# Attention with compressive memory, then a gated feed-forward block: the last steps of the blocks beside the attention are tied behind its last weighting of values

## The chip, the cores and the metric

One core of a Trainium2 chip. The metric is the device time of one execution in microseconds; of several runs the median is given. The profile is of one further execution of the same program. TensorE (PE) has two clock levels, 1.2 and 2.4 GHz; where the profile gives a granted clock, 1.00 is the higher and 0.50 the lower.

## The reference

Inputs are q, k and v of shape (4, 8, 576, 64) in float32, a memory M_prev and z_prev for each head, a gate beta for each head, and three weight matrices.

```python
scores = scale * np.matmul(q, k.transpose(0, 1, 3, 2))      # causal mask, softmax
local = np.matmul(a, v)
q_p = np.where(q > 0, q, np.exp(q) - 1.0) + 1.0
mem_out = einsum('bhsd,bhde->bhse', q_p, M_prev) / (einsum('bhsd,bhd->bhs', q_p, z_prev)[..., None] + 1e-06)
x = g * mem_out + (1 - g) * local                           # g = sigmoid(beta)
x = x.transpose(0, 2, 1, 3).reshape(2304, 512)
out = (silu(x @ w_gate) * (x @ w_val)) @ w_out              # d_ff = 1536
```

## The kernel before, in words

The attention handles sixteen pairs of heads (`Pair`, n = 0 to 15; four pairs make one batch of 576 tokens). Each pair is cut into steps: a1 and a2 make scores and their exponentials, b1 and b2 weight and transpose them, c1 and c2 multiply with the values, d1 and d2 add the part recalled from memory and store x. Every fp32 operand of PE is split into two parts, high and low, so each product takes three matmuls. The list STEPS writes out in which order the steps of pair n and of pair n - 1 are issued; a scheduler then sets the order on each engine by priorities and by its own estimate of times.

x goes to two tensors in memory outside the core, xdh and xdl (`store`, L628), as high and low parts, since the feed-forward block needs all heads of a token. It is loaded back by `load_x` (L190).

The feed-forward block is cut in two. Of its twelve slices of 128 hidden columns the first four (FC1) are done **beside the attention** for tokens 0 to 1535: `moe1` (L216), six blocks of N1 = 256 tokens. A block is ten steps: eight of `up` (L197, twelve matmuls of 256 columns each: gate for slices 0 and 1, value for 0 and 1, the same for 2 and 3), and two of `down` (L210; four slices, three matmuls of 512 columns each), whose sum is scaled by ScalarE (L248) into a tile o, of which there is one, and stored as a partial sum in `part` (L249, on SyncE's queue). Between up and down ScalarE takes Silu (L229), VectorE multiplies (u, L236), GpSimd rounds to the high part (u1h) and VectorE makes the low part (u1l). Steps are issued by `fill` (L641): at each of three places of a pair's round it issues steps up to

```python
want = math.floor(steps * (n * 3 + k - START) / (END - START))
```

with priority P_BES behind the attention; what is left at the end is issued in the loop `for _ in bgen` (L680). A block needs x of its whole batch: blocks 0 and 1 that of batch 0, blocks 2 and 3 that of batch 1 too, blocks 4 and 5 that of batch 2 too.

The **second phase** (L707) takes six chunks of 384 tokens: first the two chunks of tokens 1536 to 2303 with all twelve slices, then the four others with the last eight slices, adding the partial sums. Its weights are loaded and converted by `weights` (L163) on ScalarE and VectorE from the end of the attention on. Its first x, tiles xbh and xbl, are loaded as soon as the first 256 tokens of the last pair are stored (d1 of pair 15). PSUM banks are shared: the second phase's up uses s, g, m and av, its down tr.

Of the kernel before, what the change touches and what calls it, by code (L numbers as in the profile page):

```python
# [20 lines left out]
NP = B * NPAIR  # L21
# [6 lines left out]
N2 = 384  # L28
NT1 = 1536
WSTEP = {2: (0,), 3: (1, 2), 4: (3,)}  # L30
START, END = 14, 53
AHEAD = 1

RANK = {"recall": -50, "c1": 50, "load": 400}
# [26 lines left out]
def attention_moe(ctx: ExitStack, tc: tile.TileContext, qt, kt_, v, m, beta, wg, wv, wo, out):  # L61
    nc = tc.nc
    PE, ACT, DVE, POOL, SP = nc.tensor, nc.scalar, nc.vector, nc.gpsimd, nc.sync
# [12 lines left out]
    part = dram.tile([NT, DM], F32, name="part")  # L76
# [81 lines left out]
            DVE.tensor_copy(gx[rows, :, 4, j], gp[rows, :, j])  # L158
            DVE.tensor_copy(oy[rows, :, 8], sp[rows, :, j])

    wsplit = {}

    def weights(f, wpool, spool, tag, nraw, ntmp, after=None):  # L163
        hi = wpool.tile([128, 1536], F32R, name=f"wh{f}")
# [32 lines left out]
    def up(ps, f, gv, xh, xl):  # L197
        hi, lo = wsplit[f]
        n = 0
        for kk in range(NPAIR):  # L200
            c = slice(gv * 512 + kk * 128, gv * 512 + kk * 128 + 128)
            for wt, xx in ((hi, xh), (hi, xl), (lo, xh)):
                PE.matmul(ps, wt[:, c], xx[:, kk, :], start=(n == 0), stop=(n == 11))  # L203
                n += 1

    def gated(u, g, val):
# [2 lines left out]

    def down(ps, f, uh, ul, first, last):  # L210
        hi, lo = wsplit[f]
        PE.matmul(ps, uh, hi[:, 1024:1536], start=first, stop=False)  # L212
        PE.matmul(ps, uh, lo[:, 1024:1536], start=False, stop=False)  # L213
        PE.matmul(ps, ul, hi[:, 1024:1536], start=False, stop=last)  # L214

    def moe1(pool, t0):  # L216
        held = xb
        if t0 // N1 % 2:
            held = [rot(pool, f"bx{part}", [128, NPAIR, N1], F32R, 1) for part in "hl"]
        xh, xl = load_x(held, t0, N1)  # L220
        us = []
        for f0 in range(0, FC1, 2):
            n = min(2, FC1 - f0)
            g = rot(psG, "g", [128, 512], F32, PS_G).rearrange("p (f c) -> p f c", f=2)
            for f in range(f0, f0 + n):
                up(g[:, f - f0, :], f, 0, xh, xl)
                yield
            u = rot(pool, "u1", [128, 2, N1], F32, 1)
            ACT.activation(u[:, 0:n], g[:, 0:n], AF.Silu, scale=W_ONE)  # L229
            ps = rot(psM, "m", [128, 512], F32, PS_M).rearrange("p (f c) -> p f c", f=2)  # L230
            for f in range(f0, f0 + n):
                up(ps[:, f - f0, :], f, 1, xh, xl)
                yield
            uh = rot(pool, "u1h", [128, 2, N1], F32R, (FC1 + 1) // 2)
            ul = rot(pool, "u1l", [128, 2, N1], F32R, (FC1 + 1) // 2)
            DVE.scalar_tensor_tensor(  # L236
                out=u[:, 0:n], in0=ps[:, 0:n], scalar=W_ONE, in1=u[:, 0:n], op0=ALU.mult, op1=ALU.mult
            )
            split_hi(uh[:, 0:n], u[:, 0:n])
            split_lo(ul[:, 0:n], u[:, 0:n], uh[:, 0:n], "u1")  # L240
            us += [(uh[:, f], ul[:, f]) for f in range(n)]
        for j in range(N1 // 128):
            c = slice(j * 128, j * 128 + 128)
            ps = rot(psM, "m", [128, 512], F32, PS_M)
            for f, (uh, ul) in enumerate(us):
                down(ps, f, uh[:, c], ul[:, c], f == 0, f == FC1 - 1)
            o = rot(pool, "o1", [128, 512], F32, 1)
            ACT.mul(o, ps, W_ONE)  # L248
            SP.dma_start(part[t0 + j * 128 : t0 + j * 128 + 128, :], o)  # L249
            yield  # L250

    xb = [xbp.tile([128, NPAIR, N2], F32R, name=f"xb{part}") for part in "hl"]
# [8 lines left out]
    with tc.tile_pool(name="sb", bufs=1, reuse_waits="tile") as sb:  # L261
# [62 lines left out]
        class Pair:  # L324
# [270 lines left out]
            def c2(self):  # L595
                if self.plain:
                    av = rot(psA, "av", [128, 512], F32, PS_A)[:, 0:320]
                    g = self.g2[0]
                    for kk in range(5):
                        o = max(0, (kk - 2) * 128)  # L600
                        for h in range(2):
                            PE.matmul(  # L602
                                av[:, o:320], self.vz[:, kk, h, :], g[:, kk, h, o:320] if kk < 4 else self.last_keys(g, h),
                                start=(kk == 0 and h == 0), stop=False,
                            )
                    self.recalled(av, 2, 3)
                    self.give(2, av)
                    return
                x = self.x2 = rot(quick[0], "x2", [128, 320], F32, 2)
                for h in range(2):  # L610
                    av = rot(psA, "av", [128, 512], F32, PS_A)[:, 0:320]
                    for kk in range(5):
                        o = max(0, (kk - 2) * 128)
                        for g in self.g2:
                            keys = g[:, kk, h, o:320] if kk < 4 else self.last_keys(g, h)
                            PE.matmul(  # L616
                                av[:, o:320], self.vs[:, h, kk, :], keys,
                                start=(kk == 0 and g is self.g2[0]), stop=(kk == 4 and g is self.g2[1]),
                            )
                    self.joined(x, av, h)  # L620

            def d2(self):
                if not self.plain:
# [59 lines left out]
    with tc.tile_pool(name="stg2", bufs=1, reuse_waits="tile") as stg2, \  # L683
# [23 lines left out]
        for t0 in [N2 * i for i in ORDER]:  # L707
# [21 lines left out]
            for f in fs:  # L729
                pp = []  # L730
                for gv in range(2):
                    ngv[0] += 1
                    ps = banks[nj + ngv[0] % (len(banks) - nj)]
# [75 lines left out]
```

## Time and profile before

| | us |
|---|---|
| median of 3 runs (749.72 to 752.3) | 751.47 |
| the profiled execution | 753.47 |
| its span, first to last instruction | 751.7 |

| engine | busy, us | share of the span |
|---|---|---|
| PE | 693.1 | 92% |
| DVE (VectorE) | 401.7 | 53% |
| ACT (ScalarE) | 332.4 | 44% |
| POOL (GpSimd) | 197.9 | 26% |

The attention ends near 390 us, and what follows is the second phase. Busy time of PE is the time in which a matmul is in work; successive matmuls overlap, so the spacing of their starts tells how fast they go. "L203" is line 203 of the kernel. A wait is named by the instruction that waited and the one that released it.

### The profile page before, as it was taken

The numbers are of one execution on the slowest core, as the hardware profiler recorded it, in microseconds if no ns is written. First come the engines' busy times: TensorE is split into PE (matmuls) and PEld (weight loads), VectorE is DVE, ScalarE is ACT, GpSimd is POOL, SyncE is SP. The second block draws the span as 40 slices with busy tenths as digits, with TensorE's granted clock in tenths as the row PEclk, the third lists the DMA queues.
The fourth block names the chain that finished last, engine by engine and source line by source line (L and its number), as shares of the span: only waits on it lengthen the run. The fifth ranks groups of instructions, "written<-read, shape, count | busy, mean of one in ns | idle before, by whom it ended". The sixth has DMA issues, their size and how long they took to land.

```text
span 751.7 us, 11326 instructions
## 1 busy us (share of the span) xinstructions
PE 693.1 (92%) x4172; PEld 621.6 (83%) x4172; DVE 401.7 (53%) x1042; ACT 332.4 (44%) x737; POOL 197.9 (26%) x264
## 2 busy tenths in 40 slices
PE   4577798999979999899969999999999999999997
PEld 2466676998769997698859999999999999999996
DVE  8887764776876977775736995111111221211212
ACT  5555455667668686576725663211121111111111
POOL 5885943544444553452300000000000000000000
PEclk9789799999989999899988999999999999999999
DMA  9555144230362312401048760300040310400201
GB/s 262 180 169 148 54 124 150 70 114 19 104 197 88 114 39 78 162 33 61 20 156 295 221 226 26 115 1 1 13 156 1 112 57 0 169 1 1 84 1 43
DMA packets 43928, 72.58 MB, mean 97 GB/s; under 512 B 11744, under 2 KB 24544, under 8 KB 43872
## 3 DMA queue, kind: packets, MB, share of 16 engines
q1 hardware_dynamic: 43728, 71.56, 29.4%
q8 instruction: 33, 0.54, 0.3%
q10 hardware_dynamic: 144, 0.29, 0.1%
q14 instruction: 23, 0.19, 0.1%
HBM read 54.54 MB, written 17.30 MB: 96 GB/s over the span
## 4 chain that ended last, share of the span: by engine, by line
PE 70%; DVE 11%; DMA 8%; ACT 6%; issue 2%; POOL 2%; SPq 0%; DVEq 0%; ACTq 0%; POOLq 0%
PE s L203 13%; PE g L203 9%; PE m L203 8%; PE av L203 6%; PE tr L213 5%; PE tr L212 5%; PE tr L214 5%; PE s L396 3%; PE av L616 2%; PE tr L473 2%; DMA xbl<-xdl 2%; PE av L602 2%; PE m L212 2%; DMA xbh<-xdh 1%; PE m L213 1%
## 5 line engine op out<-in xcount | busy, mean ns | idle before, releaser
L743 ACT CAST uh<-u 128x384 fp32r<-128x384 f32 x56 | 28.8, 514 | 109.8 <-DVE u L738 109.8
L213 PE MATMUL tr<-wl,uh 128*128 128x512 f32 x168 | 66.5, 396 | 0.0
L212 PE MATMUL tr<-wh,uh 128*128 128x512 f32 x168 | 66.1, 393 | 0.0
L214 PE MATMUL tr<-wh,ul 128*128 128x512 f32 x168 | 64.7, 396 | 0.0
L738 DVE SCALAR_TENSOR_TENSOR u<-s,u 128x384 f32<-128x384 f32 x23 | 12.8, 557 | 86.9 <-PE s L203 86.9
L396 PE MATMUL s<-kh,qh 64*128 64x128 f32 (+3 forms) x128 | 31.1, 463 | 28.8 <-DVE mx L406 15.2
L410 ACT ACTIVATE pl<-pl,mx 128x384 f32<-128x384 f32 (+1 forms) x64 | 42.6, 667 | 31.3 <-DVE mx L406 31.2
L449 POOL TENSOR_SCALAR pl<-pl,rs 128x384 f32<-128x384 f32 (+1 forms) x64 | 44.4, 712 | 19.9 <-ACT x L500 10.8
L396 PEld LDWEIGHTS s<-kh,qh 64*128 64x128 f32 x128 | 14.0, 207 | 40.3 <-DVE mx L406 18.6
L111 DVE TENSOR_TENSOR ul<-u,uh 128x384 fp32r<-128x384 f32 x56 | 31.2, 557 | 26.7 <-ACT uh L743 26.7
L111 DVE TENSOR_TENSOR g2l<-tr,g2h 128x512 fp32r<-128x512 f32 (+1 forms) x66 | 36.2, 572 | 17.1 <-ACT g2h L455 16.4
L449 POOL TENSOR_SCALAR ps<-ps,rs 128x128 f32<-128x128 f32 (+1 forms) x64 | 27.9, 454 | 61.2 <-DVE rs L446 26.4
L473 PE MATMUL tr<-ident,pl 128*128 128x128 f32 x224 | 39.9, 316 | 3.5 <-POOL pl L449 2.0
L406 DVE CUSTOM_DVE_ANT_0 pl<-s,maskp 128x384 f32<-128x384 f32 (+1 forms) x64 | 37.7, 618 | 9.9 <-PE s L396 9.9
L473 PEld LDWEIGHTS tr<-ident,pl 128*128 128x128 f32 x224 | 29.3, 161 | 10.4 <-POOL pl L449 4.5
L214 PEld LDWEIGHTS tr<-wh,ul 128*128 128x128 f32 x168 | 31.6, 188 | 7.3
L203 PE MATMUL s<-xbh,wh 128*128 128x384 f32 x92 | 32.1, 352 | 4.9 <-DMA xbh<-xdh 4.9
L212 PEld LDWEIGHTS tr<-wh,uh 128*128 128x128 f32 x168 | 31.6, 188 | 5.2
L213 PEld LDWEIGHTS tr<-wl,uh 128*128 128x128 f32 x168 | 31.6, 188 | 5.1
L410 ACT ACTIVATE ps<-ps,mx 128x128 f32<-128x128 f32 (+1 forms) x64 | 28.9, 452 | 13.3 <-DVE mx L406 13.1
L455 ACT CAST g2h<-tr 128x512 fp32r<-128x512 f32 (+1 forms) x66 | 30.5, 494 | 7.0 <-PE tr L473 4.8
L737 ACT ACTIVATE u<-s 128x384 f32<-128x384 f32 x23 | 11.2, 489 | 49.5 <-PE s L203 49.5
(197 smaller groups left out, 2188.2 us busy)
## 6 DMA issues: line engine op xcount, KB each, us to landing
qr<-in_qt_dram SPq DMA_DIRECT2D x16, 384.0 KB, 4.2
out_dram<-pt SPq DMA_DIRECT2D x18, 256.0 KB, 2.2
kr<-in_kt_dram SPq DMA_DIRECT2D x15, 288.0 KB, 3.8
xdh<-xh SPq DMA_DIRECT2D x15, 288.0 KB, 2.6
xdl<-xl SPq DMA_DIRECT2D x15, 288.0 KB, 2.2
wrawb<-in_wg_dram SPq DMA_DIRECT2D x8, 512.0 KB, 4.1
wrawb<-in_wv_dram SPq DMA_DIRECT2D x8, 512.0 KB, 4.4
wrawb<-in_wo_dram SPq DMA_DIRECT2D x8, 512.0 KB, 4.3
```

Of the source, the lines that this page charges most:

```text
L111: return eng.tensor_tensor(dst, src, hi.bitcast(F32), op=ALU.subtract)
L203: PE.matmul(ps, wt[:, c], xx[:, kk, :], start=(n == 0), stop=(n == 11))
L212: PE.matmul(ps, uh, hi[:, 1024:1536], start=first, stop=False)
L213: PE.matmul(ps, uh, lo[:, 1024:1536], start=False, stop=False)
L214: PE.matmul(ps, ul, hi[:, 1024:1536], start=False, stop=last)
L396: mm = PE.matmul(ps[h][:, 0:w], q[rows, t * 128 : t * 128 + 128], k[rows, 0:w], start=(i == 0), stop=(i == 2))
L406: read[id(ps[h])] = DVE.tensor_tensor_reduce(out=p[:, 0:w], in0=ps[h][:, 0:w], in1=maskp[:, 512 - w : 512], op0=ALU.add, op1=ALU.min, scal ...
L410: ACT.activation(p[:, 0:w], p[:, 0:w], AF.Exp, bias=mx[:, c + h : c + h + 1], scale=-1.0, accum_out=self.sm[:, c + h : c + h + 1],)
L449: POOL.tensor_scalar(p, p, rs[:, i : i + 1], 1.0, op0=ALU.mult, op1=ALU.mult)
L455: ACT.copy(view(g[0]), src)
L473: PE.transpose(tr[:, c * 128 : c * 128 + 128], p[:, (k0 + c) * 128 : (k0 + c) * 128 + 128], ident)
L743: ACT.copy(uh, u)
```

## The change

Three things are changed. END goes from 53 to 56, so that `fill` issues the sixty steps over more of the attention. The last matmul of the last pair's c2 is kept (`ends`), and each sum of `up` and each first matmul of `down` that is written after it follows it in PE's order. These are steps 48 to 59, the two downs of block 4 and all of block 5, and also all of the second phase. The store of the partial sum is issued by ScalarE instead of SyncE.

```diff
-START, END = 14, 53
+START, END = 14, 56
...
-    wsplit = {}
+    wsplit, ends = {}, []
...
             for wt, xx in ((hi, xh), (hi, xl), (lo, xh)):
-                PE.matmul(ps, wt[:, c], xx[:, kk, :], start=(n == 0), stop=(n == 11))
+                mm = PE.matmul(ps, wt[:, c], xx[:, kk, :], start=(n == 0), stop=(n == 11))
+                if n == 0 and ends:
+                    follow(mm, ends[-1], "kept for the time that the last x takes to come back")
                 n += 1
...
     def down(ps, f, uh, ul, first, last):
         hi, lo = wsplit[f]
-        PE.matmul(ps, uh, hi[:, 1024:1536], start=first, stop=False)
+        mm = PE.matmul(ps, uh, hi[:, 1024:1536], start=first, stop=False)
+        if ends:
+            follow(mm, ends[-1], "kept for the time that the last x takes to come back")
...
             ACT.mul(o, ps, W_ONE)
-            SP.dma_start(part[t0 + j * 128 : t0 + j * 128 + 128, :], o)
+            ACT.dma_start(part[t0 + j * 128 : t0 + j * 128 + 128, :], o)
...
                         for g in self.g2:
                             keys = g[:, kk, h, o:320] if kk < 4 else self.last_keys(g, h)
-                            PE.matmul(
+                            mm = PE.matmul(
                                 av[:, o:320], self.vs[:, h, kk, :], keys,
...
                     self.joined(x, av, h)
+                if self.n == NP - 1:
+                    ends.append(mm)
```

The scheduler makes a new order of it. Lines of the changed file are some four to six higher than those of before (L620 is L616 before, L214, L217 and L218 are L212 to L214, L477 is L473, L505 is L501, L240 is L236). Numbers behind a name tell buffers apart.

PE, the last pair's transposes of weighted exponentials (tr from p and pl) before, with the end of block 5's first down ahead and the start of its second behind them:

```order
L212 MATMUL m_1119<-wh_870,u1h_1437 128x512
L213 MATMUL m_1119<-wl_871,u1h_1437 128x512
L214 MATMUL m_1119<-wh_870,u1l_1438 128x512
L473 MATMUL tr_254<-ident,p_220 128x128 x4
L473 MATMUL tr_249<-ident,pl_202 128x128 x4
L473 MATMUL tr_259<-ident,p_220 128x128
L212 MATMUL m_1119<-wh_505,u1h_1262 128x512
L213 MATMUL m_1119<-wl_506,u1h_1262 128x512
L214 MATMUL m_1119<-wh_505,u1l_1263 128x512
```

The same place on PE in the changed kernel:

```order
L477 MATMUL tr_249<-ident,pl_357 128x128 x3
L477 MATMUL tr_254<-ident,p_220 128x128 x4
L477 MATMUL tr_259<-ident,pl_369 128x128 x4
L477 MATMUL tr_249<-ident,pl_202 128x128 x4
L513 MATMUL tr_254<-ident,mem_159 128x128 x2
L516 MATMUL tr_254<-fold,mem_159 128x64
L620 MATMUL av_275<-g2h_1229,vs_982 128x320
L477 MATMUL tr_259<-ident,p_220 128x128
L620 MATMUL av_275<-g2l_1230,vs_982 128x320
```

Before, twelve matmuls of down stood on either side of these transposes; now none does, and from the last pair's first scores on PE has the attention's matmuls alone.

PE, the last weighting of values (av, pair 15) and what follows it, before:

```order
L616 MATMUL av_275<-g2h_1229,vs_982 128x320
L616 MATMUL av_275<-g2l_1230,vs_982 128x320
L616 MATMUL av_275<-g2h_1229,vs_982 128x192
L616 MATMUL av_275<-g2l_1230,vs_982 128x192
L616 MATMUL av_275<-g2h_1229,vs_982 128x64
L616 MATMUL av_275<-g2l_1230,vs_982 128x64
L203 MATMUL s_170<-xbh,wh_505 128x384
L203 MATMUL s_171<-xbh,wh_505 128x384
L203 MATMUL g_1042<-xbh,wh_676 128x384
L203 MATMUL m_1119<-xbh,wh_676 128x384
L203 MATMUL av_275<-xbh,wh_699 128x384
L203 MATMUL s_170<-xbl,wh_505 128x384
```

The same place in the changed kernel:

```order
L620 MATMUL av_275<-g2h_1229,vs_982 128x320
L620 MATMUL av_275<-g2l_1230,vs_982 128x320
L620 MATMUL av_275<-g2h_1229,vs_982 128x192
L620 MATMUL av_275<-g2l_1230,vs_982 128x192
L620 MATMUL av_275<-g2h_1229,vs_982 128x64
L620 MATMUL av_275<-g2l_1230,vs_982 128x64
L214 MATMUL m_1173<-wh_505,u1h_1262 128x512
L217 MATMUL m_1173<-wl_506,u1h_1262 128x512
L218 MATMUL m_1173<-wh_505,u1l_1263 128x512
L214 MATMUL m_1173<-wh_676,u1h_1262 128x512
L217 MATMUL m_1173<-wl_677,u1h_1262 128x512
L218 MATMUL m_1173<-wh_676,u1l_1263 128x512
```

Before, the second phase's matmuls with xbh stood right behind; now twelve of down and 24 of up come first, then two with xbh, then the next twelve of down, and the rest of block 5 stands among the second phase's first matmuls.

VectorE behind the attention's last instruction (xl), before, where u_3850 is the second phase's u and web, wab and wl are conversions of its weights:

```order
L111 TENSOR_TENSOR xl_443<-x_1325,xh_442 128x320
L738 SCALAR_TENSOR_TENSOR u_3850<-s_171,u_3850 128x384
L177 TENSOR_SCALAR web_3817<-web_3817 128x512
L179 TENSOR_SCALAR wab_3820<-web_3817 128x512
L111 TENSOR_TENSOR ul_3853<-u_3850,uh_3851 128x384
L180 SCALAR_TENSOR_TENSOR wab_3820<-wrawb_3815,wab_3820 128x512
```

And in the changed kernel, where u_1171 is block 5's u:

```order
L111 TENSOR_TENSOR xl_443<-x_1313,xh_442 128x320
L177 TENSOR_SCALAR web_3817<-web_3817 128x512
L179 TENSOR_SCALAR wab_3820<-web_3817 128x512
L180 SCALAR_TENSOR_TENSOR wab_3820<-wrawb_3815,wab_3820 128x512
L177 TENSOR_SCALAR web_3827<-web_3827 128x512
L179 TENSOR_SCALAR wab_3830<-web_3827 128x512
L111 TENSOR_TENSOR wl_3814<-wab_3820,wh_3813 128x512
L180 SCALAR_TENSOR_TENSOR wab_3830<-wrawb_3825,wab_3830 128x512
L177 TENSOR_SCALAR web_3817<-web_3817 128x512
L179 TENSOR_SCALAR wab_3820<-web_3817 128x512
L240 SCALAR_TENSOR_TENSOR u_1171<-m_1173,u_1171 128x512
```

Block 5's first u now stands behind nine conversions of weights, where before u of block 5 stood among the attention's instructions.

## Rows read from the trace of the kernel before

**Rows 1.** The page: busy time of PE (share of the span, instructions), and the granted clock of PE in 40 equal slices of the span, in tenths.

```profile
PE 693.1 (92%) x4172; PEld 621.6 (83%) x4172; DVE 401.7 (53%) x1042; ACT 332.4 (44%) x737; POOL 197.9 (26%) x264
PEclk9789799999989999899988999999999999999999
```

**Rows 2.** Busy time by stretches: the stretch and its length, then for PE, PE's weight loads, DVE, ACT and POOL the busy time (and instructions), then PE's granted clock, the share of the DMA engines and GB/s.

```profile
347.70:362.82 15.12, 15.12 (x107) 12.98 (x107) 9.98 (x33) 11.28 (x27) 3.40 (x7) 1.00 0.16 57
...
347.70:386.72 39.02, 37.38 (x264) 33.03 (x263) 25.26 (x72) 24.37 (x53) 7.45 (x13) 1.00 0.16 58
386.72:391.60 4.88, 0.00 (x0) 0.00 (x1) 1.48 (x3) 0.88 (x2) 0.00 (x0) 0.85 0.73 209
391.60:401.00 9.40, 8.64 (x27) 8.13 (x28) 0.00 (x0) 1.92 (x3) 0.00 (x0) 0.53 0.81 278
401.00:420.00 19.00, 19.00 (x102) 17.79 (x102) 18.11 (x39) 12.33 (x23) 0.00 (x0) 1.00 0.79 274
420.00:751.70 331.70, 327.04 (x1722) 305.23 (x1720) 96.52 (x182) 74.07 (x142) 0.00 (x0) 1.00 0.20 65
```

**Rows 3.** PE's instructions in order of time: start and duration in us, then line, operation and tiles, and in brackets the idle time ahead of it with its releaser. The 512-key scores of the last pair, the last weighting of values, and the second phase's start.

```profile
362.82 0.50 PE L396 MATMUL s<-kh,qh 64*128 64x512 f32 x2
...
385.20 0.41 PE L616 MATMUL av<-g2h,vs 128*128 128x320 f32 x1 [1.03 <-DVE x L501]
...
386.44 0.28 PE L616 MATMUL av<-g2l,vs 128*128 128x64 f32 x1
391.60 1.01 PE L203 MATMUL s<-xbh,wh 128*128 128x384 f32 x2 [4.89 <-DMA xbh<-xdh]
...
401.00 0.34 PE L203 MATMUL g<-xbl,wh 128*128 128x384 f32 x1
...
402.91 0.34 PE L203 MATMUL m<-xbl,wh 128*128 128x384 f32 x1
```

**Rows 4.** SyncE's DMA queue in order of time, start and duration of the issue: the first of the last x's stores, and the first load of the second phase's x.

```profile
385.06 0.32 SPq L630 DMA_DIRECT2D xdh<-xh  x1
...
386.84 0.52 SPq L193 DMA_DIRECT2D xbh<-xdh  x1
```

**Rows 5.** The chain of waits that ends last, in order of time: start, us, what.

```profile
330.36 0.71 PE m L203 x6
...
367.36 1.28 ACT L229
...
368.65 0.60 ACT u L229
...
369.27 1.28 ACT L433
...
375.50 0.50 PE m L212
375.99 0.23 PE m L213
...
378.57 0.98 PE tr L473 x9
...
382.35 1.12 PE av L616 x9
```

**Rows 6.** Instructions of single lines in the stretch from the last pair's first scores to the end of the last weighting of values: for L203 and for L212 the busy time (and count) of PE and of its weight loads, then clock, DMA share and GB/s; for L236 that of DVE.

```profile
347.70:386.72 39.02, 11.64 (x75) 9.82 (x75) 1.00 0.16 58
...
347.70:386.72 39.02, 5.03 (x12) 2.25 (x12) 1.00 0.16 58
...
347.70:386.72 39.02, 1.36 (x2) 1.00 0.16 58
```

**Rows 7.** Instructions of POOL, ACT and DVE in the last pair, in order of time by engine: POOL's five weightings, two of ACT (a cast of transposed weights, a copy between heads), two of DVE (a remainder, a sum between heads).

```profile
372.03 2.48 POOL L449 TENSOR_SCALAR pl<-pl,rs 128x384 f32<-128x384 f32 x4 [9.29 <-ACT x L500]
374.48 0.97 POOL L449 TENSOR_SCALAR p<-p,rs 128x576 f32<-128x576 f32 x1
...
376.19 0.59 ACT L455 CAST g2h<-tr 128x512 fp32r<-128x512 f32 x1
...
384.21 0.42 ACT L500 COPY x<-av 64x320 f32<-64x320 f32 x1 [1.18 <-PE av L616]
...
378.30 0.69 DVE L111 TENSOR_TENSOR g2l<-tr,g2h 128x512 fp32r<-128x512 f32 x1
...
384.67 0.48 DVE L501 TENSOR_TENSOR x<-av,x 64x320 f32<-64x320 f32 x1
```

**Rows 8.** PE's waits from 110 to 386.7 us: who waited for whom, us in total, times, longest.

```profile
PE s L396 <- DVE mx L406: 7.3, 5, 2.4
PE g L203 <- DMA xbh<-xdh: 2.8, 2, 2.0
```

**Rows 9.** DMA issues of two lines: queue, count, ns min/median/max, first and last start. The stores of partial sums on SyncE's queue, and the one load that ScalarE issues.

```profile
L249 SPq DMA_DIRECT2D part<-o x12: 319/320/412, 157.5 to 383.1; - x12
...
L271 ACTq DMA_DIRECT2D kr<-in_kt_dram x1: 402/402/402, 0.7 to 0.7; - x1
```

**Rows 10.** Busy time by stretches of 5 us, columns as in rows 2.

```profile
110.00:115.00 5.00, 3.40 (x25) 2.71 (x23) 4.93 (x12) 3.50 (x8) 4.75 (x4) 1.00 0.57 181
...
300.00:305.00 5.00, 2.75 (x20) 2.03 (x20) 4.94 (x17) 3.25 (x11) 5.00 (x6) 0.98 0.30 109
305.00:310.00 5.00, 4.67 (x22) 4.01 (x24) 4.14 (x14) 3.18 (x11) 2.49 (x6) 0.50 0.93 292
```

## The prediction

> **What bounds the kernel now.** I read the page first, then busy time by stretches, then PE's instructions at the seam between the attention and the second phase, the chain of waits ahead of it, and last the attention's own engines. The page says that PE is busy 92% of the span at a clock of nearly full [rows 1]: time can come only from PE's holes and from matmuls at the lower clock. The stretches say where: from 420 us on PE works 327.04 of 331.70 us, and from 347.70 to 386.72 us 37.38 of 39.02; but from 386.72 to 391.60 it does nothing, and from 391.60 to 401.00 it issues 27 matmuls in 9.40 us at a granted clock of 0.53 [rows 2]. PE's rows show the seam: after the last weighting of values ends (386.72) PE waits 4.89 us for xbh [rows 3], since the first of the last x is stored at 385.06 and its loads are issued from 386.84 on [rows 4]. At the full 2.4 GHz eleven such matmuls take 1.91 us (401.00 to 402.91 [rows 3]), so 27 would take 4.7 us: the second phase, ready at 401.00 with 27 matmuls done, is where it would be had it begun at 396.3 at full clock. **The seam costs 396.3 - 386.7 = 9.6 us.** The part at half clock (1.2 GHz) follows PE's idle wait and lasts until the clock returns.
>
> **The change, part by part.** It does not remove work; it moves matmuls of the blocks beside the attention.
>
> *What is held back.* The ties reach the last 12 of 60 steps: the two downs of block 4 and all of block 5, 96 matmuls of up and 48 of down. An up takes 0.71/6 = 0.118 us, a down 0.23 us [rows 5], so 96 x 0.118 + 48 x 0.234 = **22.5 us of PE work, put behind the last weighting.** Before, PE did all of it earlier: by the order, 21 ups and 12 downs stand ahead of the last pair's first scores (347.70 us), which is 2.5 + 2.8 = 5.3 us, and 75 ups and 36 downs between there and the last weighting (75 in L203's row and 12 in L212's, which has one of three lines of down [rows 6]), 8.8 + 8.4 = 17.2 us.
>
> *What that frees.* Ahead of the last pair's scores PE is full, so **-5.3 us**. In the last pair's stretch it is not that simple: 39.0 us hold 17.2 of moved work, but the attention also has DVE, ACT and POOL to wait for. Call the stretch's length without the moved work T.
> T is at least what DVE must do: 25.26 us busy [rows 2], less the two u (L236, 1.36 [rows 6]) and as much for their remainders (u1l), which go, is 22.5; the second head's last weighting, 1.5 us (385.20 to 386.72 [rows 3]), and the copy and sum between the heads, 0.42 + 0.48 [rows 7], hardly lie beside DVE's other work: low bound 25.
> At most it is what it is now less what the chain shows as moved work in its path: Silu between two table loads, 1.28 + 0.60 + 1.28, of which I count 2 us in the exponential's way, and 24 downs between 375.50 and 382.35, of which I count 4 in the way of transposes and weighting [rows 5]: 39.0 - 6 = 33.
> Between them I walk the chain in two pieces. From the first scores to the 512-key scores DVE has 9.98 us [rows 2], less one u and half a u1l, 9: with a microsecond of waits, 10. From there it took 9.2 us to POOL's first weighting (362.82 [rows 3] to 372.03 [rows 7]), 7.2 without the Silu; then POOL's five, 2.48 + 0.97 [rows 7], the transposes 0.98 [rows 5], a cast and a remainder, 0.59 + 0.69 [rows 7], the first head's weighting 1.5, copy and sum 0.9, the second's 1.5: 17.8, and 0.7 for what stands on DVE's and ACT's queues in between: 18.5. **T = 28.5**, nearer the low end because nearly all of DVE's work there has its place: -10.5 us.
>
> *What comes after.* +22.5 us of moved work, and the x, some 5 to 8 us away, comes back beside it: the seam's **-9.6 us** go, the half clock with it if PE does not stop.
> The new wait is DVE's: nine conversions of weights now stand ahead of the first u (L240 in the changed file). 39 instructions in 18.11 us [rows 2] make 0.46 each, so some 4.3 us after the first weight has landed; PE has the four groups of downs and ups and a few of the second phase to do meanwhile. Bounds 0 (all hidden) and 5 (u late by all nine, with the wait for the third weight); I take **+2**.
>
> *Spread.* END 56 puts 9.5 and 6.6 us of filling instead of 7.9 and 4.4 into the pairs' periods where x of the third batch is not yet back, and 7.8 instead of 6.2 at the second's. PE waits there now: 7.3 us for minima and 2.8 for x [rows 8]. Bounds: 5 us gained, 2 lost (less filling elsewhere); taken **-2**.
>
> *Stores.* Twelve issues move from SP to ACT; an issue on ACT took 0.402 us, on SP 0.320 [rows 9]. Twelve are 4.8 us of ACT, whose busy time is below half; four of them come after the attention. Cover: PE's filling, and DVE as the fuller engine. Without cover 4.8 us would be lost; I count 0. SP's queue loses waits that nobody needed: its x stores go out as xh and xl are ready.
>
> **Sum:** -5.3 - 10.5 + 22.5 - 9.6 + 2 - 2 = **-2.9 us**, or T - 31.4. The profiled execution took 753.47 us for a span of 751.7, the median of the runs is 751.47; 0.4% of either is the same 2.9, so 748.5 us. Below 0.3%, 2.25 us, a measurement cannot tell this kernel from itself.
>
> **Rivals.**
> *The attention's end stays long (slower).* Without filling the last pair runs at the pace of its chain. The price is one microsecond for each of T above 31.4; from 33.7 it is slower by over 0.3%. For it: PE's holes in 300 to 305 us, where there is no filling, leave PE at 2.75 of 5.00 with DVE at 4.94 [rows 10]. Against it: the table loads and downs in the chain [rows 5]. With T = 35, 755.1 us.
> *The clock falls in the thin end.* From 300 us PE worked 2.75 of 5 us and was then granted 0.50 for 305 to 310 us; from 110 us it worked 3.40 of 5 us at 1.00 [rows 10]. So a thin stretch goes either way. A fall like that of 305 us lasts some 6 us and costs 3; one in the end and one that reaches into the moved work: -2.9 + 6 = +3, 754.6 us; with one alone no change.
> On this the Trainium skill (TensorE: Matmul & The Clock Gate, "A second HAM failure mode: psum-queue depth-cycling") says that a PE which idles briefly but often between groups of matmuls swings between the two rates and loses throughput at every turn. By that the end would swing, as this rival has it; the rows at 110 us speak against it, those at 300 us for it.
> *The end closes up (faster still).* T = 25, DVE packed: -6.4, 745.1 us. Against: every pair has waits on DVE now.
> *It cancels.* T = 30 to 32 with no help from the spread, or x's loads now share the DMA engines with the weights' loads, which are issued right behind them, and come late: within 0.3%, about 751 us. The change then does not do what it says: PE waits for u or x behind the moved work instead.
>
> **How the numbers follow.** Forecast (T near 28.5) 0.37; closes up 0.10; cancels 0.25; clock 0.13, half of it the even one; end stays long 0.15. Faster by over 0.3%: 0.47; within: 0.32; slower: 0.21. The range goes from the closed end with a little more from the spread, 743.5, to T = 35 with an ACT queue somewhat late, 756.5.
>
> **What would show it.** PE without a hole of over 1 us in the 15 us after the last weighting, at clock 1.00; the last weighting near 370 us instead of 386.7; from the last pair's first scores to it 28.5 us (31.4 and above refutes the gain); no Silu table load in that stretch; twelve stores on ACT's queue with no wait for them behind. It is wrong if PE waits 5 us or more for DVE's u, if half clock covers more than 6 us of the stretch, or if the holes between 110 and 320 us have grown.

## The result, and the profile after

| | before | the change |
|---|---|---|
| median, us | 751.67 (4 runs, 749.72 to 752.30) | 761.92 (4 runs, 760.95 to 763.51) |
| ratio, 95% interval | | 1.0143 [1.0116, 1.0170] |
| the profiled execution / its span | 753.47 / 751.7 | 760.95 / 759.2 |

The change is slower by 10.2 us of median; the prediction said 748.5, 743.5 to 756.5. The two profiles differ by 7.5 us: the profiled execution of the kernel before is slower than its four runs, that of the change is the fastest of its four, so 2.7 us of the medians' difference are not in the rows below.

The page, as [rows 1]:

```profile
PE 699.0 (92%) x4172; PEld 623.7 (82%) x4172; DVE 402.2 (53%) x1042; ACT 327.5 (43%) x733; POOL 200.4 (26%) x264
PEclk9899798999989999889998999999999999999999
```

Busy time by stretches, columns as in [rows 2]: pair 14's period, with two pieces of it; the last pair, from its first scores to the last weighting; and what follows.

```profile
324.43:346.31 21.88, 19.85 (x134) 17.15 (x133) 16.84 (x52) 14.42 (x34) 8.93 (x13) 0.84 0.08 28
335.00:340.00 5.00, 3.21 (x15) 1.94 (x13) 3.85 (x11) 4.22 (x13) 1.87 (x5) 0.67 0.02 5
340.00:345.00 5.00, 5.00 (x30) 4.90 (x28) 3.42 (x11) 2.79 (x7) 0.38 (x1) 0.65 0.00 0
346.31:373.29 26.98, 23.04 (x168) 19.00 (x168) 23.72 (x75) 17.02 (x46) 8.73 (x15) 1.00 0.15 55
373.29:400.00 26.71, 26.71 (x175) 25.37 (x175) 15.69 (x31) 13.31 (x21) 2.65 (x2) 1.00 0.77 269
400.00:405.00 5.00, 3.18 (x13) 2.12 (x13) 4.97 (x12) 2.86 (x5) 0.00 (x0) 1.00 0.69 226
405.00:410.00 5.00, 2.08 (x8) 1.48 (x7) 3.13 (x7) 2.57 (x5) 0.00 (x0) 0.84 0.92 261
410.00:415.00 5.00, 5.00 (x17) 5.00 (x17) 5.00 (x12) 3.40 (x8) 0.00 (x0) 0.50 0.48 157
420.00:759.20 339.20, 334.50 (x1758) 311.79 (x1756) 86.22 (x160) 69.18 (x134) 0.00 (x0) 1.00 0.17 57
```

Behind the last weighting PE has no idle time for 26.7 us: the wait for x of 4.89 us and the half clock behind it are gone, as forecast. But two new thin places stand there, one ahead (335 to 345 us, granted clock 0.67 and 0.65, mostly the lower level) and one behind (400 to 415 us: 4.7 us without a matmul, then clock 0.50). PE's rows at both, as in [rows 3]:

```profile
336.56 0.94 PE L477 MATMUL tr<-ident,p 128*128 128x128 f32 x4 [1.31 <-DVE rs L446]
337.15 0.56 PE L203 MATMUL m<-xbh,wl 128*128 128x256 f32 x1
...
338.52 0.80 PE L400 MATMUL s<-kh,qh 64*128 64x512 f32 x2 [0.47 <-DVE mx L410]
...
373.01 0.28 PE L620 MATMUL av<-g2l,vs 128*128 128x64 f32 x1
373.12 0.48 PE L214 MATMUL m<-wh,u1h 128*128 128x512 f32 x1
...
378.83 0.51 PE L203 MATMUL s<-xbh,wh 128*128 128x384 f32 x2
...
403.30 0.50 PE L214 MATMUL m<-wh,u1h 128*128 128x512 f32 x1 [1.82 <-ACT o L252]
...
409.28 0.69 PE L203 MATMUL m<-xbh,wh 128*128 128x384 f32 x1 [2.92 <-ACT o L252]
```

337.15 us is the last untied step: from there to 373.12 PE has the attention alone, 36 us and not the 27 of the last pair. Behind, x is there without a wait (378.83), and what PE waits for is o, ScalarE's copy of a sum out of the one bank m. ScalarE's rows tell why o is late (start, duration, line; in brackets the idle time ahead and its releaser):

```profile
376.20 0.60 ACT L252 ACTIVATE o<-m 128x512 f32<-128x512 f32 x1 [0.92 <-PE m L218]
376.83 0.33 ACTq L253 DMA_DIRECT2D part<-o  x1
...
383.93 0.60 ACT L252 ACTIVATE o<-m 128x512 f32<-128x512 f32 x1 [4.30 <-DMA part<-o]
384.42 0.67 ACT L176 ACTIVATE web<-wrawb 128x512 f32<-128x512 f32 x1
...
403.28 0.33 ACTq L253 DMA_DIRECT2D part<-o  x1
...
405.68 0.69 ACT L176 ACTIVATE web<-wrawb 128x512 f32<-128x512 f32 x1 [1.36 <-DMA wrawb<-in_wv_dram]
...
408.63 0.60 ACT L252 ACTIVATE o<-m 128x512 f32<-128x512 f32 x1 [1.74 <-DMA part<-o]
```

There is one tile o. The second o of a block waits until the first has landed in memory, and ScalarE executes in order: from 379.6 to 383.93 nothing else starts there, and no weight is converted. The chain of waits names the landings (start, us):

```profile
376.83 7.01 DMA part<-o
...
403.28 5.27 DMA part<-o
```

Before, the twelve stores landed within 2.0 to 4.1 us and nobody waited for one. Here they meet the loads of x and of the weights. SyncE's queue in the change (before, its first load of weights was issued at 395.35):

```profile
371.54 0.32 SPq L636 DMA_DIRECT2D xdh<-xh  x1
...
373.37 0.52 SPq L193 DMA_DIRECT2D xbh<-xdh  x1
...
376.21 0.43 SPq L170 DMA_DIRECT2D wrawb<-in_wg_dram  x1
```

The Trainium skill (DMA: Bandwidth & Descriptors, "Anatomy of one DMA") gives a transfer on GpSimd's path some 2 us and its bytes at 436 GB/s; an estimate from that for 256 KB is 2.6 us. These stores go by SyncE's and ScalarE's queues. The trace before is near the estimate (2.0 to 4.1, median 2.8), the two landings here are not (7.0 and 5.3), and the measured times decide.

**One ledger for all runs.** Idle time alone misses what PE loses while matmuls run wider apart or at half clock. So below, "lost" is the length of a stretch less the sum, over PE's rows in it, of the shortest usual spacing of each shape in these traces (0.12 us for 128x256, 0.17 for 128x384, 0.23 for 128x512, and so on for the attention's). The work is the same in every kernel, so losses compare. The columns of stretches are us lost. Summed over a kernel's stretches they follow the spans of the profiles to about 1 us (1.6 at the worst, e8), so smaller differences in them say nothing.

| kernel | ratio to before | ahead of pair 14 | pair 14 | last pair | from the last weighting to 420 us |
|---|---|---|---|---|---|
| before | | 127.7 | 4.9 | 8.4 | 10.0 |
| the change | 1.0143 | 128.8 | 9.0 | 11.5 | 8.7 |
| difference | | +1.1 | +4.1 | +3.1 | -1.3 |

The sum, +7.0, is nearly all of the profiles' 7.5.

### The profile page after: what moved, and what is told of

Its sections match the earlier page's. It is cut to its first block, busy times and chain, and to the rows that moved or that the text cites. A ratio compares the mean times of both kernels' runs of the same rounds, so it can differ in the third digit from the quotient of the medians.

```text
span 759.2 us, 11325 instructions
## 1 busy us (share of the span) xinstructions
PE 699.0 (92%) x4172; PEld 623.7 (82%) x4172; DVE 402.2 (53%) x1042; ACT 327.5 (43%) x733; POOL 200.4 (26%) x264
## 3 DMA queue, kind: packets, MB, share of 16 engines
q1 hardware_dynamic: 42000, 68.41, 27.5%
## 4 chain that ended last, share of the span: by engine, by line
PE 66%; DVE 14%; DMA 7%; ACT 5%; issue 4%; POOL 3%; SPq 0%; POOLq 0%; DVEq 0%; ACTq 0%
PE s L203 12%; PE g L203 9%; PE m L203 8%; PE av L203 6%; PE tr L217 5%; PE tr L214 5%; PE tr L218 5%; PE s L400 3%; PE av L620 3%; PE tr L477 2%; DMA xbh<-xdh 2%; PE av L606 2%; DMA part<-o 2%; DVE x L505 1%; PE tr L372 1%
## 5 line engine op out<-in xcount | busy, mean ns | idle before, releaser
L217 PE MATMUL tr<-wl,uh 128*128 128x512 f32 x168 | 66.5, 396 | 0.0
L214 PE MATMUL tr<-wh,uh 128*128 128x512 f32 x168 | 66.1, 393 | 0.0
L218 PE MATMUL tr<-wh,ul 128*128 128x512 f32 x168 | 64.1, 396 | 0.0
L400 PEld LDWEIGHTS s<-kh,qh 64*128 64x128 f32 x128 | 13.4, 203 | 38.2 <-DVE mx L410 16.8
L477 PE MATMUL tr<-ident,pl 128*128 128x128 f32 x224 | 39.0, 306 | 5.5 <-DVE mem L386 2.4
L477 PEld LDWEIGHTS tr<-ident,pl 128*128 128x128 f32 x224 | 27.7, 155 | 13.3 <-issue 5.5
L218 PEld LDWEIGHTS tr<-wh,ul 128*128 128x128 f32 x168 | 31.6, 188 | 7.3
L459 ACT CAST g2h<-tr 128x512 fp32r<-128x512 f32 (+1 forms) x66 | 31.1, 493 | 11.9 <-PE tr L477 10.1
L214 PEld LDWEIGHTS tr<-wh,uh 128*128 128x128 f32 x168 | 31.6, 188 | 5.2
L217 PEld LDWEIGHTS tr<-wl,uh 128*128 128x128 f32 x168 | 31.6, 188 | 5.1
L203 PE MATMUL m<-xbh,wh 128*128 128x256 f32 (+1 forms) x96 | 31.3, 326 | 2.9 <-ACT o L252 2.9
```

The costliest lines, as they stand in the source:

```text
L203: mm = PE.matmul(ps, wt[:, c], xx[:, kk, :], start=(n == 0), stop=(n == 11))
L214: mm = PE.matmul(ps, uh, hi[:, 1024:1536], start=first, stop=False)
L400: mm = PE.matmul(ps[h][:, 0:w], q[rows, t * 128 : t * 128 + 128], k[rows, 0:w], start=(i == 0), stop=(i == 2))
L459: ACT.copy(view(g[0]), src)
L477: PE.transpose(tr[:, c * 128 : c * 128 + 128], p[:, (k0 + c) * 128 : (k0 + c) * 128 + 128], ident)
```

## The experiments

Each is timed against runs of the kernel before on the same chip. First the three parts of the change apart.

**e4_spread_only**, END 56 alone:

```diff
-START, END = 14, 53
+START, END = 14, 56
```

> The kernel before with END 56 alone, no ties, stores on SyncE. Theory: the spread moves 1 to 3 us of filling between periods that lose as much as they gain (up to 300 us the changed kernel lost 117.6 us of PE's time and the one before 117.9): 752 us, within 1.5. Rival: more filling waits for x of the third batch at 300 to 310 us, where the change lost 0.9 us more: 754 us or more.

Measured: 0.9936 [0.9904, 0.9968], 748.57 us: faster, below both theories. Lost: 131.2 ahead of pair 14 (3.5 more), then 5.3 and 7.7, and behind the last weighting 2.8 instead of 10.0. SyncE's row of the last x's first store:

```profile
382.81 0.32 SPq L630 DMA_DIRECT2D xdh<-xh  x1
```

And PE's rows at the seam:

```profile
388.60 0.28 PE L616 MATMUL av<-g2l,vs 128*128 128x64 f32 x1
389.33 0.62 PE L203 MATMUL s<-xbh,wh 128*128 128x384 f32 x2 [0.46 <-DMA xbh<-xdh]
...
391.86 0.44 PE L203 MATMUL s<-xbl,wh 128*128 128x384 f32 x1 [1.38 <-DMA xbl<-xdl]
```

The last x's first part is stored 6 us ahead of the last weighting's end; before it was 1.7 (385.06 and 386.72 [rows 3, 4]). Nothing was tied; block 5's last down had merely come to stand behind that x in PE's order.

**e5_act_only**, the stores alone:

```diff
-            SP.dma_start(part[t0 + j * 128 : t0 + j * 128 + 128, :], o)
+            ACT.dma_start(part[t0 + j * 128 : t0 + j * 128 + 128, :], o)
```

> The kernel before with the stores of the partial sums on ScalarE, END 53, no ties. The changed kernel stood 0.85% (6 us) above the same kernel with the stores on SyncE, of which its profile shows 2 us behind the last weighting. Theory A (ScalarE's issues cost by themselves, eleven of them among the attention's activations): 754.5 us, 2 to 3 us above before. Theory B (they cost only where something waits for o behind the attention): 752 us, within 1.5.

Measured: 0.9941 [0.9915, 0.9966], 748.48 us, below both theories. Again the seam: the x's store at 382.18, the last weighting's end near 388.1, 3.5 us lost behind it.

**e6_spread_act**, both of these and no ties.

> The kernel before with END 56 and the stores on ScalarE, no ties: the change without its ties. END 56 alone gave 0.9936 of before (747 to 748 us), since the first of the last x was stored 6 us ahead of the last weighting's end instead of 1.7. Theory A as for the run with the stores alone: 750 to 751 us. Theory B: 748 us, within 1.5. Either way the ties would stand for the rest of the change's 762: 11 to 14 us.

Measured: 0.9990 [0.9965, 1.0014], 752.56 us, above both theories. The seam is cured here as well (3.6 lost), but 132.2 are lost ahead of pair 14 and 7.4 in it; why, stays open. The gains of e4 and e5 are both the seam's and don't add. From here to the change's 1.0143 are 1.5%, 11.5 us: **the price of the ties**.

**e10_one_down**, the seam's order by itself: in the kernel before, `down` takes the last of the two transposes that finish the last pair's first x, and only the last down follows it:

```diff
-    def down(ps, f, uh, ul, first, last):
+    def down(ps, f, uh, ul, first, last, behind=None):
...
-        PE.matmul(ps, uh, hi[:, 1024:1536], start=first, stop=False)
+        mm = PE.matmul(ps, uh, hi[:, 1024:1536], start=first, stop=False)
+        if behind is not None:
+            follow(mm, behind, "behind the first x of the last pair")
...
+                     ends[0] if t0 == NT1 - N1 and j == 1 else None)
```

> The kernel before with one move: block 5's last down (12 matmuls, 2.8 us) stands behind the transposes with which the last pair's first x is finished (L509 of before), and no longer ahead of them. The order is else the same, END 53, stores on SyncE. Theory (before, those 12 matmuls stood between the last pair's first x and its store, and PE had nothing to do while x went out and came back; the runs with END 56 alone and with the stores on ScalarE alone were 0.9936 and 0.9941 since the scheduler happened to put them behind): the store 2.9 us earlier, the stretch behind the last weighting loses 3 to 4 us instead of 10.0, 748 us (746.5 to 750). Rival (those two runs gained elsewhere): 752.5 us, within 1.5.

Measured: 0.9984 [0.9965, 1.0004], 751.47 us: outside the theory's range and inside the rival's, and no gain that is clear of 1. The store went out only some 4 us ahead of the end, and PE still waited, first for the parts of the weighting and then for x:

```profile
380.80 0.41 PE L621 MATMUL av<-g2h,vs 128*128 128x320 f32 x1 [0.18 <-ACT g2h L458]
381.53 0.41 PE L621 MATMUL av<-g2l,vs 128*128 128x320 f32 x1 [0.31 <-DVE g2l L111]
...
391.14 0.62 PE L203 MATMUL s<-xbh,wh 128*128 128x384 f32 x2 [2.78 <-DMA xbh<-xdh]
...
393.89 0.69 PE L203 MATMUL s<-xbl,wh 128*128 128x384 f32 x1 [1.60 <-DMA xbl<-xdl]
```

The loss behind the last weighting fell from 10.0 to 7.5 us. In the rows the direction is right and the size wrong: with the down out of the way the first x, which stands behind the weighting in PE's order, waits for VectorE's and ScalarE's parts of it instead.

**e11_end50_only** and **e14_two_downs**: END 50 in the kernel before, and END 50 with both downs of block 5 behind that transpose.

```diff
-START, END = 14, 53
+START, END = 14, 50
```

```diff
-                     ends[0] if t0 == NT1 - N1 and j == 1 else None)
+                     ends[0] if t0 == NT1 - N1 else None)
```

> The kernel before with END 50 alone: no ties, stores on SyncE, one tile o. By its order the last down stands behind the transposes of the last pair's first x, too. Theory (the seam's cure needs no tie, and END 50 has its own gain at the third batch's x, where the run with four tied steps and END 50 lost 4.8 us in 300 to 320 us instead of 9.8): the seam 3 to 4 us instead of 10.0, the third batch's x 3 to 5 us less: 744 us (742 to 748). Rival (the four ties made that run's gain): 750 us or more.

> The kernel before with END 50, and both downs of block 5 (24 matmuls, 5.6 us) behind the transposes that finish the last pair's first x; no tie to the last weighting, stores on SyncE, one tile o. In the runs so far the time between the issue of that x's store and the end of the last weighting, and what PE loses from there to 420 us, went 1.7 and 10.0, 3.8 and 7.5, 4.7 and 6.9, 5.8 and 3.5, 6.1 and 2.8 us. Theory (that lead alone sets the seam): END 50 alone has 4.7, this some 7.5, which leaves 1 to 2 us of the 6.9; 740 us (738 to 742.5). Rival (END 50's order is as good as any): 744 us, within 1.5.

Measured: 0.9877 [0.9833, 0.9921], 743.69 us, and 0.9860 [0.9827, 0.9893], 741.64 us. Both lie in their theories' ranges and beat both kernels; between the two the intervals don't decide. In e11 the seam still lost 6.9 us, where 3 to 4 were expected; 121.9 were lost ahead of pair 14 (127.7 before). Of those 5.8 us some 3.6 stand in pair 13's period, at the third batch's x, in 300 to 310 us, where before PE fell to half clock [rows 10]:

```profile
300.00:305.00 5.00, 2.97 (x22) 1.99 (x21) 4.91 (x17) 4.28 (x11) 0.00 (x0) 1.00 0.71 225
305.00:310.00 5.00, 4.90 (x34) 3.86 (x35) 4.19 (x13) 3.35 (x11) 1.63 (x4) 1.00 0.97 320
```

In e14 the seam has one wait left (its profiled execution, 746.13 us, is the slowest of its six):

```profile
389.39 0.44 PE L203 MATMUL s<-xbl,wh 128*128 128x384 f32 x1 [1.26 <-DMA xbl<-xdl]
```

The time from the first x's store to the last weighting's end, and the loss behind it, in the seven kernels without ties to that end (by the end of PE's last row of it): 1.7 and 10.0 (before), 4.0 and 7.5 (e10), 4.9 and 6.9 (e11), 6.0 and 3.5 (e5), 6.1 and 3.6 (e6), 6.1 and 2.8 (e4), 7.3 and 2.4 us (e14). The longer the lead, the less is lost at the seam; e10 and e14, which move nothing but downs, lie on the same line. That the kernel's time follows as well is not shown by them: neither is clear of the kernel that it was made from.

Then the ties. **e3_end53** (the change with END 53, so eight tied steps) and **e9_tie_last4** (the change with only the last four tied: the kept matmul goes into `ends` five steps later):

```diff
-        for _ in bgen:
-            pass
+        for i, _ in enumerate(bgen):
+            if i == 4:
+                ends.append(kept_mm[0])
```

> The changed kernel with END 53 again: eight steps are tied (14.1 us of PE work) instead of twelve (22.6), pair 14's period has 12.2 us of filling as before the change and not 5.7, the last pair's 3.2 instead of 17.3 before and 0 in the change. Theory (what was lost in the attention is the thin stretch 333 to 346 us, which the last pair's own 26.9 us do not pay for): last weighting near 376 us, 14.1 us behind it, some 5 us lost there: 750 us (747 to 753). Rival (each tied microsecond costs alike, 10.2 for 22.6): 758 us.

> The change, but only block 5's last two ups and its two downs (8.4 us of PE work) are tied behind the last weighting; END 56, stores on ScalarE, one tile o as in the change. Pair 14's period has 10.5 us of filling (5.7 in the change, 12.1 before), the last pair's 9.3 (0 and 17.3). Theory (the number of tied steps thins the attention): 751 us, 0.998 of before (748 to 754). Rival (any tie brings the wait for the stored o and the late u behind the attention, and that is the price): 757 us or more.

Measured: 1.0050 [1.0017, 1.0082], 756.56 us, and 1.0110 [1.0039, 1.0180], 760.88 us. In e3 the time lies above its theory's range and below its rival's 758; e9 came out as its rival had it, at 757 or more. Fewer ties did not repair it. Each against its own kernel without ties, twelve tied steps cost 1.5% (the change and e6), eight 1.1% (e3 and e5) and four 1.2% (e9 and e6). In e3 pair 14 is whole (4.5 lost) but the last pair loses 14.0; in e9, 8.4 and 11.9. In both a part ran at half clock; e9's two periods:

```profile
326.00:353.11 27.11, 25.71 (x187) 23.00 (x186) 18.10 (x57) 18.50 (x39) 8.89 (x13) 0.94 0.06 23
353.11:387.85 34.74, 30.70 (x212) 26.77 (x212) 25.16 (x72) 20.28 (x48) 9.65 (x16) 0.95 0.17 59
```

And 7.4 us go behind the last weighting with only 8.4 us of work there: this is the late o of e9's rival. ScalarE, with block 5's o and the second phase's Silu in its order behind conversions:

```profile
395.60 0.66 ACT L176 ACTIVATE web<-wrawb 128x512 f32<-128x512 f32 x1 [5.76 <-DMA wrawb<-in_wg_dram]
```

Last, what holds o. **e1_two_o** (the change with two tiles o; a second time as **e1_again**, whose rows are used here), **e2_sp_store** (the change with the stores on SyncE), **e7_sp_two_o** (both), **e12_late_weights** (e2 with the weights' loads behind the last store of a partial sum) and **e13_both** (e12 with two tiles):

```diff
-            o = rot(pool, "o1", [128, 512], F32, 1)
+            o = rot(pool, "o1", [128, 512], F32, 2)
```

```diff
-            SP.dma_start(part[t0 + j * 128 : t0 + j * 128 + 128, :], o)
+            stores[:] = [SP.dma_start(part[t0 + j * 128 : t0 + j * 128 + 128, :], o)]
...
-                yield from weights(f, w2, stg2, "b", 4, 2)
+                yield from weights(f, w2, stg2, "b", 4, 2, stores[0])
```

> The changed kernel with two tiles o in place of one (the order on every engine stays, but for the buffers). Theory: behind the last weighting, ScalarE stands at the second o until the first partial sum has landed (7.0 us for 256 KB among the loads of x and weights), and again at the last o (5.3 us); the conversions of weights and block 5's u stand behind it. With two tiles both waits go: of the 8.6 us that the stretch from the last weighting to 420 us now loses, some 5 come back, 757 us (755 to 759). Rival: u is late since the conversions of weights stand ahead of it on VectorE and ScalarE whatever o does; then 762 us, within 1.5.

> The change with two tiles o, once more, for its profile. Theory (a single tile o on ScalarE's own queue holds that queue until the partial sum lands): ratio to before near 1.008 as in its first timing, and no wait of o for a partial sum in the profile; ScalarE then waits for the weights instead, and the stretch behind the last weighting loses some 7 us instead of 8.7. Rival (the first timing was chance): ratio 1.013 or more.

> The changed kernel with the stores of the partial sums back on SyncE, one tile o. Theory (the tile o is what is waited for): the wait for the landing stays, 762 us, within 2. Rival (the issue on ScalarE holds its queue): the conversions start some 4 us earlier, 757 us.

> The change with the stores on SyncE (1.0058 of before, 757 us) and two tiles o. There ScalarE waits 3.50 and 1.01 us for a partial sum's landing, but the first weights land at 380.8 us, 0.2 us behind the first of these waits' end. Theory (the weights' loads are as late as the store): 1 us back at most, 756 us (754.5 to 757.5). Rival (the tile is what holds the stretch): 4 us back, 753 us.

> The change with the stores on SyncE (1.0058 of before, 757 us), and the second phase's loads of weights held on SyncE's queue until the last partial sum is stored, so that neither the stores' landing nor block 5's u and o meet them. Theory (behind the attention, block 5's chain of u, high part, low part, down, o and store is held up by the weights' loads and conversions): the 6.6 us lost there fall to some 3, 754 us (752 to 755.5). Rival (the conversions then come late for the second phase's fifth slice): 758 us or more.

> The change with the stores on SyncE, with two tiles o and with the weights' loads held behind the last partial sum, both. With two tiles alone the stretch behind the last weighting lost 7.1 us, since ScalarE then stood at conversions that wait for weights; with late weights alone 6.3, since it stood at o for the landing of a partial sum (3.09 and 4.68 us), with the second phase's Silu behind it. Theory (either wait covers for the other): together the stretch loses 2 to 3 us, 752.5 us (751 to 754.5). Rival (the stretch is block 5's chain itself, in which nothing but the next instruction's latency is waited for): 757 us, within 1.5.

| kernel | ratio to before | ahead of pair 14 | pair 14 | last pair | behind |
|---|---|---|---|---|---|
| e1, again | 1.0083 [1.0056, 1.0109], 1.0099 [1.0064, 1.0135] | 130.0 | 8.7 | 11.5 | 7.4 |
| e2 | 1.0058 [1.0032, 1.0085] | 128.4 | 6.5 | 11.9 | 6.6 |
| e7 | 1.0062 [1.0039, 1.0085] | 129.2 | 6.6 | 12.3 | 7.1 |
| e12 | 1.0035 [0.9996, 1.0074] | 133.0 | 7.3 | 11.8 | 6.3 |
| e13 | 1.0060 [1.0036, 1.0083] | 129.8 | 8.5 | 13.0 | 3.5 |

Of the five kernels' times only e12's lies in its theory's range, and not for its reason: 6.3 us are lost behind, not the 3 that it should have come from. e7's 757.62 is just above its range; e1's second time came out as expected, at a loss of 7.4 us behind the last weighting.

Two tiles end the wait for the landing, and the wait for weights takes its place, one instruction on. ScalarE in the second run of e1:

```profile
383.37 0.60 ACT L252 ACTIVATE o<-m 128x512 f32<-128x512 f32 x1 [2.54 <-PE m L218]
384.74 0.66 ACT L176 ACTIVATE web<-wrawb 128x512 f32<-128x512 f32 x1 [0.78 <-DMA wrawb<-in_wg_dram]
...
407.81 0.66 ACT L176 ACTIVATE web<-wrawb 128x512 f32<-128x512 f32 x1 [2.78 <-DMA wrawb<-in_wv_dram]
408.37 0.60 ACT L184 CAST wh<-wab 128x512 fp32r<-128x512 f32 x1
408.88 0.59 ACT L252 ACTIVATE o<-m 128x512 f32<-128x512 f32 x1
```

The o of 408.88 now stands behind two conversions (in the change, at 408.63, it stood behind the landing). Late weights without a second tile leave the landing's wait in e12:

```profile
409.74 0.60 ACT L252 ACTIVATE o<-m 128x512 f32<-128x512 f32 x1 [4.68 <-DMA part<-o]
```

Only both together take the loss behind the last weighting down. Busy time from there to 420 us (columns as in [rows 2]), in e7 with two tiles alone:

```profile
371.94:420.00 48.06, 44.83 (x256) 40.67 (x256) 34.80 (x70) 26.35 (x44) 2.66 (x2) 0.96 0.83 282
```

And in e13 with late weights too:

```profile
375.18:420.00 44.82, 43.40 (x256) 39.75 (x256) 11.99 (x24) 12.16 (x21) 1.24 (x2) 1.00 0.45 157
```

PE is idle for 1.42 us instead of 3.23 and the clock stays full: 3.5 us lost instead of 7.1. So what held that stretch is shown: o behind the landing and behind the weights' conversions, either covering for the other. The times did not follow it: e13 stands where e2 and e7 do, since in its profile the attention's end lost 2.6 us more than e7's, at a granted clock of 0.92 and 0.94 where e7 had 1.00. The order there is the same by steps, so I can't tell it from chance. That the stores moved back to SyncE gain 4 to 6 us (e2 against the change) only e2's rival had expected, and not for this reason: the first conversion starts 10.7 us behind the last weighting in e2 and 11.1 in the change, not 4 us earlier. In the rows the gain is 2.1 us behind the last weighting and 2.5 in pair 14, whose period is at full clock in e2 and at 0.84 in the change:

```profile
323.25:343.91 20.66, 18.79 (x147) 16.25 (x146) 18.43 (x57) 15.43 (x37) 9.55 (x13) 1.00 0.08 30
```

**e8_sp_two_end50**, four tied steps with END 50, two tiles, stores on SyncE:

> Ties, stores on SyncE, two tiles o, and END 50, so that only four steps are tied (block 5's last two ups and its two downs, 8.4 us of PE work); pair 14's period keeps 11.7 us of filling (12.1 before), the last pair's 10.5 (17.3 before). Theory (a tied microsecond beyond the some 6 us of x's way out and back buys nothing and thins the attention): the attention loses some 1 us more than before, the stretch behind it some 4 us instead of 10.0: 747 us (744 to 750). Rival (ties hurt however few, since u and o stand behind the weights' conversions): 753 us or more.

Measured: 0.9898 [0.9864, 0.9932], 745.57 us, within the theory's range, but not for its reason: 121.6 us lost ahead of pair 14 is END 50's gain, which e11 has without a tie (121.9). In the last two pairs together and behind the last weighting e8 loses 16.1 and 5.7, e11 11.8 and 6.9. Ties gain nothing there; their cost (0.9898 against e11's 0.9877) is within the intervals.

## Why the prediction was wrong

*What bounds the kernel; the seam.* Right. The seam cost some 10 us (lost: 10.0) and in the change PE waits for no x there.

*T, the last pair alone: forecast 28.5, bounds 25 and 33.* Measured 26.98 (346.31 to 373.29), DVE busy for 23.72 of it: 1.5 us better than forecast. Walking VectorE's chain was the right way to find it, but the pieces named for its second half add up to 16.8 and not 17.8: they give T = 27.5 and a sum of -3.9, so part of those 1.5 us is a slip in adding. The rival of a long end did not come.

*"Ahead of the last pair's scores PE is full, so -5.3 us", and -2 for the spread.* This step failed. The last pair's first scores came 1.4 us earlier (347.70 to 346.31), not 7.3. I had counted what is tied, but not where the untied steps run out. Priorities put filling wherever PE is free; with 12 of 60 steps held, the other 48 were done at 337.15, in the middle of pair 14. From there PE waited (1.31 and 0.47 us) and went at half clock for most of 335 to 345 us. Pair 14 had 5.7 us of filling instead of 12.1 and lost 4.1 us more. PE's order, which was at hand, would have told it, since PE's rows follow that order. Of the 4.1 us up to 3.4 are the clock: two stretches of 5 us at 0.67 and 0.65 are worth that much of work at the full clock. The last weighting came at 373.3 instead of 368.9: 4.4 of the error (5.9 from here, less the 1.5 of T). The spread's own -2 was not there: END 56 alone lost 3.5 us more ahead of pair 14.

*"+2" for what comes after the moved work.* This step failed too. From the last weighting to the end the change takes 385.9 us and the kernel before 365.0, 20.9 more where 22.5 - 9.6 + 2 = 14.9 were forecast: the term measured 8.0 instead of 2, which is 6.0 of the error. In the rows it is the 4.7 us without a matmul and some 3 (an estimate from the granted clock in 405 to 415 us) at half clock behind them. I had looked at VectorE's nine conversions ahead of u; the two u were late by them by some 1.4 us each (the first one's sums were ready near 388.2, it ran at 389.56), and PE had other work meanwhile. What PE waited for is o. I had put the stores on ScalarE at 0 with a bound of 4.8, since I counted the issues' 0.4 us and not what the next user of the tile waits for: the landing. Before, the downs of a block stood among attention work, 3.8 us apart (the two o at 378.61 and 382.44), with landings of at most 4.1; tied together behind the attention they meet the loads, and bank m, tile o and ScalarE's order are then one serial chain.

*The sum.* 4.4 + 6.0 = 10.4 above -2.9 gives the +7.5 of the profiles.

*The rivals.* Two came together that I had priced apart: the clock fell in the thin end and again in the moved work (335 to 345 and 405 to 415 us), and the change turned its wait for x into a wait behind the moved work. In pair 14 of the change PE was idle for 2.03 us of 21.88, in three stops (the longest 1.31), and the clock was 0.84; in e2 it was idle for 1.87 of 20.66, in five stops (the longest 0.96), at 1.00. The Trainium skill (TensorE: Matmul & The Clock Gate, "A second HAM failure mode: psum-queue depth-cycling") has a PE that idles briefly but often swing between the two clocks. The change's trace has one fall in that period and e2's, with more stops, none: the rule doesn't tell the two apart.

*What I did not ask.* Whether the seam needed a tie at all. [rows 3, 4] had it: the store at 385.06, the end at 386.72. Twelve matmuls of down stood ahead of the store that could stand behind it (e4, e5, e14); e10 shows that this alone gives back only a part.

Open: why pair 14 falls to half clock in some of the tied kernels and not in others; why the time did not follow where the wait for o was taken away (e13); and the 2.7 us by which the medians differ more than the profiles.

## What to carry to other kernels

To cover a round trip through memory, start the trip earlier and put some 6 us of ready work behind its start (leads of 6.0 to 7.3 us left 2.4 to 3.6 of the 10.0 lost); don't hold work back for it that is filling a stretch which others bound. When work is held back, ask where the rest of the filling then runs out. And work that was harmless when spread out becomes a serial chain when it is put together: look for its single buffers, and for the engine's in-order queue that stands behind them.

## What the runs showed of the hardware

- A store of 256 KB landed in 2.0 us at the least and in 7.0 among loads of x and weights (the change). Even with the weights held back, the last o of e12 waited 4.68 us for one.
- A wait of PE doesn't decide by itself on the clock: 1.56 and 2.07 us, three us of work between them, left it at 1.00 (e2 from 370 to 420 us, its rows below); 1.82 and 2.92 were followed by 0.50 (the change).

```profile
399.79 0.50 PE L214 MATMUL m<-wh,u1h 128*128 128x512 f32 x1 [1.56 <-ACT o L252]
...
404.92 0.44 PE L203 MATMUL m<-xbh,wh 128*128 128x384 f32 x1 [2.07 <-ACT o L252]
```

- With 23.7 us less filling (12.1 + 17.3 before, 5.7 in the change) the last two pairs' periods grew shorter by 17.3 us (66.2 to 48.9); with 8.4 less the last pair's alone (18.9 in e11, 10.5 in e8) by 4.1 (38.16 to 34.02). Work that fills gaps is not free, but it costs less than its length.
